# Hashed attention and expert layer: other layouts for turns and casts, moves and signs two pairs at a time, signs by bit operations, the uniform term by matmul

## The chip, the core and the metric

The kernel runs on one core of one Trainium2 chip. The metric is the device time of one execution in microseconds, the median of several runs. The core's engines are TensorE (PE, with PEld for its weight loads), VectorE (DVE), ScalarE (ACT), GpSimd (POOL) and SyncE (SP, which here only issues DMAs). They run side by side, each through its own list of instructions in a fixed order, and wait for one another by semaphores. An instruction that waits holds back everything behind it on its engine.

## What is computed

Attention over four batches, eight heads, 768 positions and 64 features, where a query sees only the keys with the same hash (the signs of six projections), and on its output a layer of eight low-rank experts, of which two are used per row.

```python
q_bits = (np.einsum('bhsd,dk->bhsk', q, proj) > 0)      # the same for k; 6 bits
mask = q_bucket[:, :, :, None] == k_bucket[:, :, None, :]
scores = np.where(mask, scale * np.matmul(q, k.transpose(0, 1, 3, 2)), -1e9)
attn = softmax(scores); attn_out = np.matmul(attn, v)   # exp, divided by sum + 1e-9
logits = x @ w_gate                                     # x: attn_out, 3072 x 512
# the two largest logits e, softmaxed to w:
out = x + sum_e w[e] * ((x @ A[e]) @ B[e])              # A[e]: 512x16, B[e]: 16x512
```

## The kernel before

The 32 (batch, head) problems are taken as 16 pairs `p` of heads, four pairs to a batch. The whole program is a hand-held list, `ORDER`: each word is a method and its numbers (`sc.9.2` is `sc(9, 2)`), and the list's order is the order of the instructions on every engine. No scheduler moves anything.

For each pair from 1 on, q and k come in by DMA (`l`, into `nat`, three buffers), 128 partitions of 768 floats per tensor. DVE turns them in blocks of 32x32 (`t`, L278, into `R`). POOL casts `R` to bf16 in the order in which the transposed operand needs it (`c`, L281, into `Rb`): it reads contiguously and writes every sixth bf16 element. Eight DMAs per pair (`mv`, L286) move blocks of `Rb` to their partitions in `aug`: rows 0 to 63 hold the features, one column per position. Pair 0 goes another way, without those DMAs: TensorE transposes (`ta`), copies (`tca`), casts into `aug` (`ca`, L250), hash matmuls (`ha`, L258) and signs (`sa`, L265).

The hash of a pair is eight f32 matmuls (`h`, L295, two instructions each), which read `R` with a step of 64 elements. DVE compares with zero (`sn`, L299) and scales by a per-partition number (`sm2`, L303); a DMA writes the signs to DRAM (`sdw`, L307), another reads them back as seven rows of `aug` (`sdr`, L310). The score matmul (`sc`, L339) then contracts 71 rows: 64 features, six signs of ±16 whose products add up to a large number only where all agree, and one constant row. For a mismatch the exponential of the score vanishes.

The scores are cut into 146 tiles, nine to a pair, of 1024 columns each, in three buffers of PSUM. ScalarE turns each into P (`ex`, L344, bf16, three buffers). Products with V (`pv`, L366) of a pair run among the scores of the next pair. For queries that see no key, each product starts from a tiny uniform term: POOL sums V (`vsum`, L319 to L323), TensorE spreads the sum over the rows (`uni`, L326), DVE copies it to SBUF (`ucopy`, L330) and, before each half pair, into the PSUM bank of the products (`seed`, L355). A half pair ends with `rec` and `norm` on DVE (L372, L382), which free the bank. POOL also casts V (`vcast`, L314) and the output (`xcast`, L401). The expert layer of a batch (`xturn`, `lzm`, `top`, `dif`, `sel`, `gexp`, `gate`, `zmul`, `delta`, `addx`, `store`) stands among the scores of later pairs, and for the last batch at the end. The last two pairs go in four groups of query blocks.

SP issues nearly all DMAs in list order: loads, the 120 moves, the sign transfers, the stores.

## Time and profile before

| | |
|---|---|
| time, median of 3 runs | 240.85 us (237.78 to 241.51) |
| the profiled execution | 237.42 us, span 235.6 us, mean granted clock of TensorE 0.878 |
| busy of the span | PE 184.8, DVE 159.1, ACT 147.6, POOL 162.4 us |
| the 146 exponentials (L344) | 142.9 us busy, 64.2 us idle before them |
| largest other groups | PE scores 101.5, POOL casts L281 88.5, PE products 58.4, PE hashes 33.1 us |
| DMAs issued by SP | 120 moves `aug<-Rb`, 15 `dr<-s`, 15 `aug<-dr`, 46 loads of q, k, v for pairs, stores, weights |

"Busy" is the time in which at least one instruction of the group ran. Idle time is put down to what ended it, by the semaphore that came last. The granted clock is a share of 2.4 GHz.

### The profile page before, as it was taken

How to read it: one execution, taken by the hardware profiler on the slowest of the kernel's cores; microseconds unless marked ns; L12 is line 12 of the kernel's file. 1: busy time of each engine (PE TensorE's matmuls, PEld its weight loads, DVE VectorE, ACT ScalarE, POOL GpSimd, SP SyncE). 2: the span in 40 equal slices, each digit the busy share in tenths (PEclk: the TensorE clock that was granted, in tenths of full speed). 3: DMA queues.
4: the chain of work that ended last, by engine and by line, in shares of the span. 5: the costliest groups of instructions: out<-in, count | busy, mean ns of one | idle time of the engine just before them, and what ended most of it. 6: DMA issues, size and time to landing. Idle time of an engine off the chain costs nothing.

```text
span 235.6 us, 5542 instructions
## 1 busy us (share of the span) xinstructions
PE 184.8 (78%) x2131; PEld 114.1 (48%) x2131; DVE 159.1 (68%) x364; ACT 147.6 (63%) x163; POOL 162.4 (69%) x168
## 2 busy tenths in 40 slices
...
GB/s 216 336 50 28 192 132 52 178 229 134 181 223 137 164 184 45 190 276 133 95 179 212 183 34 160 145 207 147 203 69 82 85 50 67 123 3 3 187 162 188
DMA packets 41495, 33.36 MB, mean 142 GB/s; under 512 B 25433, under 2 KB 38397, under 8 KB 41469
## 3 DMA queue, kind: packets, MB, share of 16 engines
...
HBM read 20.06 MB, written 7.03 MB: 115 GB/s over the span
## 4 chain that ended last, share of the span: by engine, by line
PE 25%; POOL 24%; DVE 18%; DMA 9%; SPq 9%; issue 9%; ACT 4%; ACTq 0%; DVEq 0%; POOLq 0%
POOL Rb L281 17%; PE s L339 10%; SPq L286 7%; PE v L366 6%; DVE aug L265 6%; ACT P L344 4%; DMA aug<-Rb 4%; PE n L295 3%; DVE acc L490 3%; POOL va L319 3%; DMA proj<-in_proj_dram 2%; DMA vn<-in_v_dram 2%; DVE R L278 2%; DMA aug<-dr 2%; POOL vs L323 1%
## 5 line engine op out<-in xcount | busy, mean ns | idle before, releaser
L344 ACT ACTIVATE P<-s 128x1024 bf16<-128x1024 f32 (+1 forms) x146 | 142.9, 1045 | 64.2 <-PE s L339 62.1
L339 PE MATMUL s<-aug 71*128 71x256 bf16 (+4 forms) x432 | 101.5, 337 | 16.3 <-DMA aug<-Rb 9.1
L281 POOL CAST Rb<-R 128x768 bf16<-128x768 f32 x30 | 88.5, 3032 | 11.5 <-DMA aug<-Rb 10.4
L339 PEld LDWEIGHTS <-aug 71*128 71x128 bf16 (+1 forms) x432 | 45.3, 130 | 59.1 <-issue 36.7
L366 PEld LDWEIGHTS <-P 128*128 128x128 bf16 x1152 | 53.7, 103 | 22.1 <-issue 13.5
L366 PE MATMUL v<-vb,P 128*128 128x65 bf16 x1152 | 58.4, 200 | 3.4 <-DVE v L355 2.0
L295 PE MATMUL n<-R,hst 128*32 128x192 f32 x240 | 33.1, 610 | 1.9 <-POOL Rb L281 1.3
L278 DVE STREAM_TRANSPOSE R<-nat 128x768 f32<-128x768 f32 x30 | 29.8, 997 | 4.1 <-POOL Rb L281 3.9
L401 POOL CAST xb<-x 128x768 bf16<-128x768 f32 (+1 forms) x18 | 13.6, 756 | 27.3 <-DVE x L382 20.3
L319 POOL TENSOR_TENSOR va<-vn 128x384 f32<-128x384 f32 x16 | 17.7, 1116 | 6.2 <-DMA vn<-in_v_dram 6.1
L490 DVE SCALAR_TENSOR_TENSOR acc<-n,rt,x 128x512 f32<-128x512 f32 x17 | 12.7, 749 | 12.6 <-PE n L486 12.1
L382 DVE TENSOR_TENSOR x<-v,ri 128x384 f32<-128x384 f32 x28 | 16.8, 600 | 0.7
L299 DVE TENSOR_SCALAR sg<-n 128x192 bf16<-128x192 f32 x15 | 5.2, 349 | 17.4 <-PE n L295 17.4
L355 DVE COPY v<-u 128x390 f32<-128x390 f32 x28 | 15.8, 564 | 0.6
L314 POOL CAST vb<-vn 128x768 bf16<-128x768 f32 x16 | 13.5, 850 | 0.7 <-PE v L366 0.7
L413 DVE COPY xT<-n 128x768 bf16<-128x768 bf16 (+1 forms) x18 | 8.7, 484 | 7.1 <-PE n L408 6.8
L250 POOL CAST aug<-R 64x128 bf16<-64x128 f32 (+2 forms) x14 | 12.3, 1010 | 0.7 <-ACT R L243 0.5
L295 PEld LDWEIGHTS n<-R,hst 128*32 128x32 f32 x240 | 7.0, 120 | 11.8 <-issue 3.5
L303 DVE TENSOR_SCALAR s<-sg,ssc 128x192 bf16<-128x192 bf16 x15 | 12.5, 833 | 0.2
L372 DVE RECIPROCAL ri<-v 128x6 f32<-128x6 f32 x28 | 6.3, 225 | 9.0 <-PE v L366 8.6
L408 PE MATMUL n<-ident_bf,xb 128*128 128x128 bf16 x92 | 8.4, 225 | 2.5 <-DVE rt L466 2.3
L326 PE MATMUL n<-vs,eps 128*128 128x130 bf16 x16 | 3.8, 238 | 7.6 <-POOL vs L323 7.0
...
## 6 DMA issues: line engine op xcount, KB each, us to landing
...
aug<-Rb SPq DMA_DIRECT2D x120, 48.0 KB
...
```

The costliest lines, as they stand in the source:

```text
L265: self.nc.vector.tensor_scalar(out=self.augt(slice(64, 82), h, i, e, u, n), in0=self.hb(h)[r, u * P:(u + n) * P].rearrange("d (u p) -> d u ...
L278: self.nc.vector.transpose(out=self.R[p % 2][:, i], in_=self.nat[p % 3][:, i])
L281: self.nc.gpsimd.tensor_copy(out=self.Rb[p % 2][:, :, i].rearrange("p h f (c t) -> p h t f c", t=T), in_=self.R[p % 2][:, i].rearrange("p ...
L286: (self.nc.sync, self.nc.gpsimd)[eng].dma_start(out=self.aug[p % 4][32 * f:32 * f + 32, :, 192 * a:192 * a + 192], in_=self.Rb[p % 2][32 * ...
L295: self.nc.tensor.matmul(out=hs[32 * j:32 * j + 32], lhsT=self.hst[:, f].rearrange("p b i -> p (b i)"), rhs=rhs, start=(f == 0), stop=(f == ...
L319: add(out=a, in0=vn[:, :, 0:3, :], in1=vn[:, :, 3:6, :])
L339: self.nc.tensor.matmul(out=self.Sb[n % 3][:, o:o + qw], lhsT=aug[rows, 2 * h + 1, kt::T], rhs=aug[rows, 2 * h, q0:q0 + qw], start=True, s ...
L344: self.nc.scalar.activation(out=self.Pt[p % 3][:, at:at + w], in_=self.Sb[n % 3][:, 0:w], func=ACT.Exp, scale=0.125)
L355: self.nc.vector.tensor_copy(out=self.pvv(p, g), in_=self.u[p % 2][:, g:g + 1, :].to_broadcast([P, T, D + 1]))
L366: self.nc.tensor.matmul(out=v[:, i, :], lhsT=self.Pt[p % 3][:, o:o + P], rhs=self.vb[p % 3][:, h, kt, :], start=False, stop=(kt == T - 1), ...
L382: self.nc.vector.tensor_tensor(out=x[:, :, c:c + D], in0=v[:, :, 0:D], in1=self.ri[g % 2].unsqueeze(2).to_broadcast([P, T, D]), op=ALU.mult)
L490: self.nc.vector.scalar_tensor_tensor(out=self.acc[(m // 2) % 3][:, m % 2, lo:hi], in0=self.bank(bank)[:, lo:hi], scalar=self.rt[g % 2][:, ...
```

## The change

- `c` walks `R` in the order of its output: it reads floats 64 elements apart and writes contiguous bf16. `h` reads runs of 32 contiguous floats and leaves its result in the order (t, c); the permutation is done by `sn`.
- `Rb` and `aug` hold two pairs per buffer (two buffers each, instead of two and four of one pair). A move and a sign transfer of an even pair carry that pair and the next; pair 1 goes alone. P has two buffers instead of three.
- Signs are made by one bit operation: the projections are negated, so a set bit is a negative number, and `bits` takes the upper half of the f32 in PSUM, keeps its sign bit and sets the other bits to 16.0. `sm2`, the constant row and the constants for them go; the scores contract 70 rows, and the exponential gets a bias of −192 (six products of 256, times 0.125).
- Pair 0 is laid out in the order in which its casts and signs come, so both write contiguously; its q is loaded in pieces of 256 bytes for that.
- The uniform term is written straight into the PSUM bank by a matmul (`uv`) before each half pair. `uni`, `ucopy` and `seed` go.
- `dif`, `sel` and `gate` are written as scalar_tensor_tensor.
- `ORDER` is another list.

```diff
-        self.Rb = r("Rb", 2, [2, 2, 2, 192], BF16)
+        self.Rb = r("Rb", 2, [2, 2, 2, 2, 192], BF16)
+        self.sg = r("sg", 2, [2, 192], U16)
+        self.aug = r("aug", 2, [8, S], BF16)
-        self.Pt = r("P", 3, [2 * T * S], BF16)
+        self.Pt = r("P", 2, [2 * T * S], BF16)
...
     def la(self, i, h, eng):
         (self.nc.sync, self.nc.scalar)[eng].dma_start(
-            out=self.natA[:, h, i], in_=self.qk[i][0, h].rearrange("(p t) d -> p (t d)", t=T))
+            out=self.natA[:, h, i].rearrange("p (t d) -> p t d", t=T),
+            in_=self.qk[i][0, h].rearrange(("(t p) d -> p t d", "(p t) d -> p t d")[i], t=T))
...
     def augt(self, rows, h, i, e, u, n):
-        return self.aug[0][rows, 2 * h + i].rearrange("d (p u e) -> d e u p", e=2, u=3)[:, e, u:u + n]
+        return self.aug[0][rows, 2 * h + i].rearrange("d (u e p) -> d e u p", e=2, u=3)[:, e, u:u + n]
...
+    def bits(self, out, in_):
+        self.nc.vector.tensor_scalar(out=out, in0=in_, scalar1=0x8000, scalar2=0x4180, op0=ALU.bitwise_and,
+                                     op1=ALU.bitwise_or)
+
     def sa(self, h, i, e, u, n):
         c = 2 * i + e
-        r = slice(32 * c, 32 * c + 18)
-        self.nc.vector.tensor_scalar(out=self.augt(slice(64, 82), h, i, e, u, n),
-                                     in0=self.hb(h)[r, u * P:(u + n) * P].rearrange("d (u p) -> d u p", u=n),
-                                     scalar1=self.thr[r], scalar2=self.mul[r], op0=ALU.is_gt, op1=ALU.mult)
+        hi = self.hb(h)[32 * c:32 * c + 6, u * P:(u + n) * P].bitcast(U16).rearrange("d (u p w) -> d u p w", u=n, w=2)
+        self.bits(self.augt(slice(64, 70), h, i, e, u, n).bitcast(U16), hi[:, :, :, 1])
...
     def c(self, p, i):
-        self.nc.gpsimd.tensor_copy(
-            out=self.Rb[p % 2][:, :, i].rearrange("p h f (c t) -> p h t f c", t=T),
-            in_=self.R[p % 2][:, i].rearrange("p h (t f c) -> p h t f c", f=2, c=32))
+        self.nc.gpsimd.tensor_copy(out=self.Rb[(p // 2) % 2][:, p % 2, :, i].rearrange("p h f (c t) -> p h f c t", t=T),
+                                   in_=self.R[p % 2][:, i].rearrange("p h (t f c) -> p h f c t", f=2, c=32))
 
     def mv(self, p, a, f, eng=0):
+        lo = 1 if p == 1 else 0
         (self.nc.sync, self.nc.gpsimd)[eng].dma_start(
-            out=self.aug[p % 4][32 * f:32 * f + 32, :, 192 * a:192 * a + 192],
-            in_=self.Rb[p % 2][32 * a:32 * a + 32].rearrange("d h i f x -> d (h i) f x")[:, :, f])
+            out=self.aug[(p // 2) % 2][32 * f:32 * f + 32, 4 * lo:8, 192 * a:192 * a + 192],
+            in_=self.Rb[(p // 2) % 2][32 * a:32 * a + 32, lo:2].rearrange("d j h i f x -> d (j h i) f x")[:, :, f])
 
     def h(self, p, f):
-        hs = self.Nb[:, 0:192].rearrange("m (c t) -> m c t", t=T)
         for j in range(4):
             h, i = divmod(j, 2)
-            rhs = self.R[p % 2][:, i, h, :].rearrange("p (t f c) -> p f c t", f=2, c=32)[:, f]
-            self.nc.tensor.matmul(out=hs[32 * j:32 * j + 32], lhsT=self.hst[:, f].rearrange("p b i -> p (b i)"),
-                                  rhs=rhs, start=(f == 0), stop=(f == 1), skip_group_check=True)
+            self.nc.tensor.matmul(out=self.Nb[32 * j:32 * j + 32, 0:192],
+                                  lhsT=self.hst[:, f].rearrange("p b i -> p (b i)"),
+                                  rhs=self.R[p % 2][:, i, h].rearrange("p (t f c) -> p f t c", f=2, c=32)[:, f],
+                                  start=(f == 0), stop=(f == 1), skip_group_check=True)
 
     def sn(self, p):
-        self.nc.vector.tensor_scalar(out=self.sg[p % 2], in0=self.Nb[:, 0:192], scalar1=0.0, scalar2=0.5,
-                                     op0=ALU.is_gt, op1=ALU.subtract)
+        hi = self.Nb[:, 0:192].bitcast(U16).rearrange("p (t c w) -> p c t w", t=T, w=2)[:, :, :, 1]
+        self.bits(self.sg[(p // 2) % 2][:, p % 2].rearrange("p (c t) -> p c t", t=T), hi)
...
+    def uv(self, p, g):
+        if p < N - 2:
+            v = self.vs[p % 2][:, g:g + 1, :].to_broadcast([P, T, D + 1])
+        else:
+            v = self.vs[p % 2].unsqueeze(2).to_broadcast([P, 2, len(GROUPS[g]), D + 1])
+        self.nc.tensor.matmul(out=self.pvv(p, g), lhsT=self.eps, rhs=v, start=True, stop=False, skip_group_check=True)
...
-        self.nc.vector.tensor_mul(out=self.sm["gw"][g % 2][:, 0:n], in0=self.sm["m"][g % 2][:, 0:n],
-                                  in1=self.sm["e"][g % 2][:, 0:n])
+        self.nc.vector.scalar_tensor_tensor(out=self.sm["gw"][g % 2][:, 0:n], in0=self.sm["m"][g % 2][:, 0:n], scalar=1.0,
+                                            in1=self.sm["e"][g % 2][:, 0:n], op0=ALU.mult, op1=ALU.mult)
...
+c.9.1 sc.50.0 rec.4.1 sc.50.1 top.0.0.0 mv.6.1.0 lzm.0.1.1.0.4.-1 norm.4.1 lzm.0.1.2.0.4.-1 c.9.0 ex.49 dif.0.0 lv.8
```

The last line is one of the new list: the last move of pairs 6 and 7 stands behind tile 49 or so; tile 54 is the first of pair 6.

Three places of the order, before and after. The first is DVE at the start, behind the copies of pair 0's transposes (`R_73`); `R_74` belongs to pair 1, `s_67` and `v` are hash results in PSUM. Before:

```order
L265 TENSOR_SCALAR aug_81<-s_67,thr,mul 18x128 x2
L278 STREAM_TRANSPOSE R_74<-nat_71 128x768
L265 TENSOR_SCALAR aug_81<-s_67,thr,mul 18x128 x4
L278 STREAM_TRANSPOSE R_74<-nat_71 128x768
L265 TENSOR_SCALAR aug_81<-s_67,thr,mul 18x128 x2
L265 TENSOR_SCALAR aug_81<-s_67,thr,mul 18x2x128 x2
L265 TENSOR_SCALAR aug_81<-v,thr,mul 18x3x128
L299 TENSOR_SCALAR sg_78<-n 128x192
L303 TENSOR_SCALAR s_80<-sg_78,ssc 128x192
L265 TENSOR_SCALAR aug_81<-v,thr,mul 18x3x128 x3
```

After:

```order
L259 STREAM_TRANSPOSE R_74<-nat_71 128x768
L242 TENSOR_SCALAR aug_79<-s_67 6x128
L259 STREAM_TRANSPOSE R_74<-nat_71 128x768
L242 TENSOR_SCALAR aug_79<-s_67 6x128 x2
L242 TENSOR_SCALAR aug_79<-s_67 6x2x128
L242 TENSOR_SCALAR aug_79<-s_67 6x128 x3
L242 TENSOR_SCALAR aug_79<-s_67 6x2x128
L242 TENSOR_SCALAR sg_77<-n 128x192
L242 TENSOR_SCALAR aug_79<-v 6x3x128 x4
```

The number of signs is the same; the second turn of pair 1 stands behind three single signs where it stood behind six, and the second operation on pair 1's signs (L303) is gone.

The second place is PE at the uniform term of pair 4 (`vs_90`, then `vs_86`). `s_65` to `s_67` are the three score buffers, `aug_84` and `aug_79` hold pair 4. Before:

```order
L339 MATMUL s_65<-aug_84 128x256
L326 LDWEIGHTS eps
L326 MATMUL n<-vs_90,eps 128x130
L339 LDWEIGHTS aug_84
L339 MATMUL s_67<-aug_84 128x256
```

After:

```order
L324 MATMUL s_67<-aug_79 128x256
L350 LDWEIGHTS eps
L350 MATMUL v<-vs_86,eps 128x390
L324 LDWEIGHTS aug_79
L324 MATMUL s_65<-aug_79 128x256
L324 LDWEIGHTS aug_79
L324 MATMUL s_67<-aug_79 128x256
L357 LDWEIGHTS P_94
L357 MATMUL v<-vb_84,P_94 128x65
```

The short matmul into the bank `n` became a wide one into the bank `v` of the products, directly ahead of the products (L357) and once for each half pair; two scores stand between.

The third place is SP, the transfers of pairs 6 and 7 (`Rb_75` into `aug_83` and `Rb_76` into `aug_84` before; `Rb_76` into `aug_80` after). Before:

```order
L286 DMA aug_83<-Rb_75 32x4x192
L286 DMA aug_84<-Rb_76 32x4x192 x2
L286 DMA aug_83<-Rb_75 32x4x192 x2
L286 DMA aug_84<-Rb_76 32x4x192
L272 DMA nat_72<-in_q_dram 128x2x384
L286 DMA aug_83<-Rb_75 32x4x192
L310 DMA aug_83<-dr_60 7x4x768
L286 DMA aug_83<-Rb_75 32x4x192
L286 DMA aug_84<-Rb_76 32x4x192 x2
```

After:

```order
L267 DMA aug_80<-Rb_76 32x8x192
L253 DMA nat_71<-in_q_dram 128x2x384
L267 DMA aug_80<-Rb_76 32x8x192 x4
L285 DMA dr_61<-sg_78 128x2x192
L267 DMA aug_80<-Rb_76 32x8x192 x2
L253 DMA nat_70<-in_q_dram 128x2x384
L290 DMA aug_80<-dr_61 6x8x768
L267 DMA aug_80<-Rb_76 32x8x192
```

Sixteen moves, two writes and two reads of signs became eight, one and one, each of twice the size.

## Rows read from the trace of the kernel before

**Rows 1.** The page, busy us (share of the span) and instructions of each engine.

```profile
PE 184.8 (78%) x2131; PEld 114.1 (48%) x2131; DVE 159.1 (68%) x364; ACT 147.6 (63%) x163; POOL 162.4 (69%) x168
```

**Rows 2.** Windows: stretch, length, busy PE PEld DVE ACT POOL, clock, DMA, GB/s.

```profile
0.00:18.00 18.00, 11.43 (x65) 4.01 (x69) 11.96 (x31) 3.21 (x8) 13.19 (x34) 0.71 0.59 197
18.00:28.80 10.80, 5.22 (x23) 2.13 (x24) 10.60 (x9) 3.98 (x4) 10.50 (x10) 0.66 0.45 119
28.80:224.00 195.20, 163.79 (x2017) 106.01 (x2015) 128.31 (x288) 139.75 (x149) 138.70 (x126) 0.91 0.48 136
224.00:235.60 11.60, 4.32 (x32) 1.96 (x32) 8.28 (x39) 0.68 (x4) 0.00 (x0) 0.73 0.47 173
```

**Rows 3.** Timeline of ACT: start us, length, instructions, [idle before <- releaser].

```profile
28.83 3.38 ACT L344 ACTIVATE P<-s 128x1024 bf16<-128x1024 f32 x3 [5.45 <-PE s L339]
...
142.29 10.32 ACT L344 ACTIVATE P<-s 128x1024 bf16<-128x1024 f32 x11 [0.67 <-PE s L339]
```

**Rows 4.** Waits within 28.8 to 224 us: total us, times, longest us.

```profile
ACT P L344 <- PE s L339: 55.0, 45, 5.4
...
PE s L339 <- DMA aug<-Rb: 9.1, 4, 3.3
...
PE n L326 <- POOL vs L323: 7.0, 4, 2.6
...
PE s L339 <- DMA aug<-dr: 4.2, 2, 3.0
...
PE v L366 <- DVE v L355: 2.0, 3, 1.1
```

**Rows 5.** Groups by line and shape: busy us, mean ns | idle before.

```profile
L281 POOL CAST Rb<-R 128x768 bf16<-128x768 f32 x30 | 88.5, 3032 | 11.5 <-DMA aug<-Rb 10.4 <-DVE gw L457 0.5 <-DVE s L303 0.3
L366 PE MATMUL v<-vb,P 128*128 128x65 bf16 x1152 | 58.4, 200 | 3.4 <-DVE v L355 2.0 <-DVE v L358 1.4
...
L355 DVE COPY v<-u 128x390 f32<-128x390 f32 x28 | 15.8, 564 | 0.6
...
L401 POOL CAST xb<-x 128x768 bf16<-128x768 f32 x14 | 12.0, 858 | 21.8 <-DVE x L382 20.3 <-PE s L339 1.6
...
L457 DVE TENSOR_TENSOR gw<-m,e 128x24 f32<-128x24 f32 x6 | 7.5, 1247 | 0.2 <-ACT e L453 0.2
...
L265 DVE TENSOR_SCALAR aug<-v,thr,mul 18x384 bf16<-18x384 f32 x4 | 6.2, 1558 | 0.1
L265 DVE TENSOR_SCALAR aug<-s,thr,mul 18x128 bf16<-18x128 f32 x8 | 6.0, 756 | 0.9 <-PE s L258 0.8
L250 POOL CAST aug<-R 64x384 bf16<-64x384 f32 x4 | 5.6, 1551 | 0.1
...
L299 DVE TENSOR_SCALAR sg<-n 128x192 bf16<-128x192 f32 x15 | 5.2, 349 | 17.4 <-PE n L295 17.4
...
L250 POOL CAST aug<-R 64x128 bf16<-64x128 f32 x8 | 4.9, 733 | 0.1
...
L326 PE MATMUL n<-vs,eps 128*128 128x130 bf16 x16 | 3.8, 238 | 7.6 <-POOL vs L323 7.0 <-DVE sg L299 0.7
...
L401 POOL CAST xb<-x 128x256 bf16<-128x256 f32 x4 | 1.6, 400 | 5.5 <-DVE x L391 2.2 <-PE n L408 1.9 <-DVE top L439 1.4
```

**Rows 6.** Timeline of PE: sets of eight f32 matmuls, columns as in rows 3.

```profile
7.01 0.42 PE L258 MATMUL s<-R,px 128*32 128x128 f32 x8 [1.14 <-DVE R L243]
...
15.12 1.17 PE L295 MATMUL n<-R,hst 128*32 128x192 f32 x8 [1.34 <-POOL Rb L281]
...
128.11 1.10 PE L295 MATMUL n<-R,hst 128*32 128x192 f32 x8
```

**Rows 7.** Windows over the three sets of rows 6, columns as in rows 2.

```profile
7.00:7.45 0.45, 0.44 (x9) 0.24 (x9) 0.16 (x1) 0.26 (x1) 0.06 (x1) 1.00 0.75 283
...
15.10:16.30 1.20, 1.17 (x8) 0.22 (x8) 1.18 (x2) 0.00 (x0) 1.14 (x2) 0.50 0.00 0
128.10:129.20 1.10, 1.10 (x10) 0.22 (x10) 1.04 (x2) 0.93 (x1) 0.56 (x1) 1.00 0.39 94
```

More of the change, by code (lines that the diff above doesn't have):

```diff
@@ L14 @@
 BF16 = mybir.dt.bfloat16
+U16 = mybir.dt.uint16
 AX = mybir.AxisListType
@@ L548 @@
-h.7.0 norm.4.1 ex.47 mv.6.2.0 sc.48.1 dif.0.0 h.7.1 sel.0.0 xcast.4.0 seed.5.0 sdr.6 sc.49.0 gexp.0.0 mv.6.2.1
-sc.50.2 ex.48 gate.0.0 sn.7 sc.50.0 zmul.0.0.0.0 sc.49.1 mv.7.3.0 gsum.0.0 t.8.1 pv.5.0.0.3 xturn.4.0.-1
-zmul.0.0.2.0 mv.7.3.1 ex.49 pv.5.0.0.4 zmul.0.0.1.0 sc.51.1 sc.50.1 xout.4.0.-1 sc.51.0 l.11.1 vcast.7 pv.5.0.0.0
-ex.50 sc.51.2 grec.0.0 mv.7.2.0 zturn.0.0.-1 pv.5.0.0.2 sc.52.0 wcast.1 zout.0.0.-1 lv.9 pv.5.0.0.1 t.9.0 ex.51
-sc.52.1 c.8.1 mv.7.1.0 pv.5.0.0.5 sc.53.2 uni.6 mv.7.0.1 rec.5.0 ex.52 ucopy.6 c.8.0 sc.54.1 norm.5.0 lv.8 sc.53.0
@@ L558 @@
-addx.0.0.2.-1 l.12.0 ex.59 sc.60.0 sc.60.2 pv.6.0.0.4 mv.8.1.1 pv.6.0.0.5 vsum.9.0 top.0.1.0 xturn.5.0.-1 sel.0.1
-dif.0.1 mv.8.2.1 ex.60 rec.6.0 sc.62.2 sc.62.0 xout.5.0.-1 mv.8.1.0 sc.62.1 sc.61.0 c.9.0 sc.61.1 norm.6.0 gexp.0.1
-h.8.0 ex.62 h.8.1 seed.6.1 mv.9.0.1 sc.63.2 gate.0.1 sc.63.1 ex.61 pv.6.1.1.1 mv.8.2.0 sn.8 zmul.0.1.2.0 sc.63.0
-pv.6.1.1.5 sm2.8 mv.8.3.0 zmul.0.1.0.0 uni.7 pv.6.1.1.2 sc.65.1 ex.63 ucopy.7 zmul.0.1.1.0 sdw.8 sc.64.0 t.10.1
-sc.64.1 l.10.0 pv.6.1.1.4 pv.6.1.1.3 ex.64 pv.6.1.1.0 mv.9.2.1 gsum.0.1 sc.65.2 sc.65.0 rec.6.1 mv.8.0.1
@@ L573 @@
-pv.8.0.0.0 ex.79 sc.78.0 t.12.0 pv.8.0.0.3 sc.78.1 vsum.11.1 sc.78.2 uni.9 sc.80.2 pv.8.0.0.2 ex.78 c.11.0
-pv.8.0.0.4 ucopy.9 sc.80.1 sc.80.0 lzm.1.0.0.0.4.-1 rec.8.0 norm.8.0 sc.82.0 vsum.10.1 ex.80 sc.82.1
-lzm.1.0.2.0.4.-1 vcast.10 seed.8.1 sc.81.2 lzm.1.0.1.0.4.-1 sc.81.0 ex.82 pv.8.1.1.3 lzo.1.0.-1 c.11.1 sc.81.1
-pv.8.1.1.2 pv.8.1.1.4 top.1.0.1 sm2.10 sc.83.1 ex.81 top.1.0.0 sc.83.0 top.1.0.2 sdw.10 sc.83.2 pv.8.1.1.0
-pv.8.1.1.1 mv.10.1.0 pv.8.1.1.5 h.11.0 ex.83 mv.10.3.1 rec.8.1 sel.1.0 dif.1.0 sc.84.0 norm.8.1 mv.10.0.0 sc.84.1
@@ L578 @@
-sc.84.2 h.11.1 gexp.1.0 seed.9.0 xcast.8.0 ex.84 sc.85.1 sdr.10 sc.86.1 gate.1.0 sn.11 sc.85.0 sc.86.2 mv.11.2.0
-zmul.1.0.0.0 sm2.11 pv.9.0.0.1 ex.85 t.12.1 sc.86.0 xturn.8.0.-1 vsum.10.2 mv.11.2.1 pv.9.0.0.4 zmul.1.0.2.0 lv.12
-pv.9.0.0.2 ex.86 xout.8.0.-1 pv.9.0.0.3 sc.87.2 zmul.1.0.1.0 l.14.0 sc.87.1 sc.87.0 c.12.0 pv.9.0.0.0 mv.11.1.0
-zturn.1.0.-1 ex.87 sc.88.0 mv.11.0.1 sc.89.0 zout.1.0.-1 sc.88.1 gsum.1.0 c.12.1 uni.10 pv.9.0.0.5 grec.1.0
-mv.11.3.0 sc.89.1 ex.88 ucopy.10 sc.89.2 rec.9.0 sdw.11 sc.90.0 norm.9.0 delta.1.0.0.-1 vsum.11.2 mv.11.3.1 sc.90.2
@@ L588 @@
-addx.1.0.2.-1 pv.10.0.0.3 ex.94 l.15.1 pv.10.0.0.4 sc.98.2 mv.12.2.0 c.13.1 sc.98.0 dif.1.1 sel.1.1 pv.10.0.0.2
-t.13.0 xturn.9.0.-1 gexp.1.1 ex.96 sc.98.1 pv.10.0.0.5 vsum.12.1 sc.97.0 gate.1.1 pv.10.0.0.1 c.13.0 gsum.1.1
-pv.10.0.0.0 xout.9.0.-1 ex.98 sc.97.1 sc.99.1 rec.10.0 sc.99.2 h.12.0 norm.10.0 zmul.1.1.2.0 mv.13.2.0 h.12.1 ex.97
-zmul.1.1.0.0 seed.10.1 mv.13.1.1 sc.99.0 sc.101.1 zmul.1.1.1.0 sn.12 sc.101.2 store.0.2.0 pv.10.1.1.1 ex.99 sm2.12
-uni.11 sc.100.1 mv.13.0.1 sc.100.0 ucopy.11 pv.10.1.1.5 mv.12.3.0 zturn.1.1.-1 ex.100 pv.10.1.1.2 sc.101.0 mv.12.0.1
```

341 lines of the change are left out of this document (169 added, 172 removed).

## The prediction

> **What bounds the kernel now.** I read the page's busy shares first, then the stages by windows, then ScalarE's timeline, the waits inside the long stage, and last the durations by shape. The shares name no single bound: PE 78%, POOL 69%, DVE 68%, ACT 63% [rows 1]. The stages do better [rows 2]. Up to 28.8 us only four of the 146 exponentials (L344) have run; DVE and POOL are busy 10.6 and 10.5 of the last 10.8 us there, and the granted clock is 0.66 of 2.4 GHz while PE is busy 5.2 us. From 28.8 to 224.0 us the other 142 run, PE busy 163.8 of 195.2 us at a mean granted clock of 0.91; the last 11.6 us are the end of the expert layer, mostly DVE. ScalarE is not the bound: once it ran eleven exponentials in 10.32 us, 0.94 each [rows 3], and 142 at that pace are 133 us of the 195. It waits 55.0 us in that stage for score matmuls [rows 4]. So PE and what feeds PE set the end: 163.8 us of PE work and 31.4 us of PE idle. Of that idle, PE's own rows name the moves of q and k into `aug` (9.1), the sign rows read back from DRAM (4.2), and the sum of V from POOL (7.0) [rows 4].
>
> The profiled execution took 237.4 us, 1.8 more than its span of 235.6. The sum is made against it; the median shown is 240.85, 1.4% above, so a median of the changed kernel may sit that much higher too.
>
> **The change, part by part.**
>
> *The start (28.8 us).* DVE's signs of pair 0 (`sa`, L265) write two-byte elements six columns apart: 756 ns for 128 columns, 1558 for 384. L299 writes 192 contiguous ones in 349, and the copy L355 writes 390 in 564 [rows 5]. The new `sa` writes contiguously, at most 0.35 and 0.56: eight and four of them fall from 12.2 us to 5.0. POOL's casts into `aug` (L250) make the same change of layout: 733 and 1551 ns, against 400 for 256 contiguous columns and 858 for 768 (L401), so 0.40 and about 0.52; 10.5 us become 5.3. The casts of pair 1 (L281) follow on POOL. Both chains shrink by 7 us or a little more, and either would end last, so I take 7.5 (4 if first loads, now in pieces of 256 bytes for q, come late; 11 if both chains and the two 256-wide forms fall together). The new order puts pair 1's turns ahead of some signs, as the old one does.
>
> *The cast `c` (L281).* 3032 ns for 768 elements, written two bytes wide and 12 bytes apart, 28 of its 30 behind 28.8 us. The new one reads four-byte elements 256 bytes apart and writes contiguously. No row of the trace has that. The bounds are 858 (L401, contiguous on both sides) and 3032 (as slow as now) [rows 5]; with one side mended I take the middle, 1.9. That frees 28 × 1.13 = 32 us of POOL's 138.7 in the stage; POOL is off PE's path except through the waits named above, so the gain is counted there. The Trainium skill (GPSIMD Engine Reference, Performance pitfalls for Q7 kernels) speaks against this edit: reads whose step is above 8 bytes cost about 2.9 cycles an element instead of 1.9. That half more, put on the 858 of the contiguous row, would give an estimate of 1.3 us and 48 us of POOL freed, and 1 us off the start; no row of this trace shows a strided read on POOL.
>
> *The hash (`h`, L295).* A set of eight takes 1.10 us at granted clock 1.00 (2.4 GHz) and 1.17 at 0.50 (1.2 GHz) [rows 6, 7]: its time does not follow the clock. The same kind of matmul on contiguous data (L258) took 0.42 for eight of 128 columns at clock 1.00 [rows 6, 7]; for 192 columns that is 0.63. The new `h` reads runs of 32 contiguous elements. 28 sets in the long stage × 0.47 = −13.2 us of PE (0 if runs of 32 do not help; −19 if 0.42 holds).
>
> *The uniform term.* `uni` (16 × 238 ns, 3.8 us [rows 5]), `ucopy` and 36 `seed` copies go; 36 `uv` matmuls come, 28 of 390 columns. Six L366 matmuls of 65 columns are as wide, at 58.4/1152 = 51 ns each [rows 5]: 0.30 us. 28 × 0.30 and eight narrower, 1.2, less 3.8, is +5.8 us of PE (0 to +8). DVE loses 15.8 us of seeds [rows 5], which nobody waited for but PE for 2.0 us [rows 4]; `uv` waits for `norm`, one step earlier, so −1.
>
> *Moves for two pairs.* 120 moves of 48 KB become 8 of 48 and 56 of 96, plus half the sign transfers. PE's waits for them are 13.3 us [rows 4]. Places where a pair can come late fall from 15 to 8, and the casts ahead of them shorten: 13.3 × 8/15 = 7.0, so −6.3 (0 to −13). The `uv` matmuls still need the sum of V; with 32 of 138.7 us taken out of POOL's queue ahead of it I take half of the 7.0, −3.5 (0 to −7).
>
> *The clock.* 0.91 leaves 9% of 163.8, 15 us, if PE's time followed it fully. Idle falls by 10.8 of 31.4, a third, so −5 (0 to −8).
>
> *The rest.* `sm2` goes, `sn` reads halves of words: DVE has 67 us idle in the stage, which hides either. The gating's new form (`dif`, `sel`, `gate`) may shorten six 1247 ns products (L457) [rows 5]; DVE's idle hides that too, and uncovered it is 7.5 us at most. Two buffers instead of three for P: V·P of a pair ends inside the next pair in the order, so nothing waits. The exponential's bias is a column read instead of a constant: nothing.
>
> Sum: 28.8 − 7.5 = 21.3; 195.2 − 13.2 + 5.8 − 1 − 6.3 − 3.5 − 5 = 172.0; 11.6 as before. That is 204.9, and with 1.8 outside the span 206.7: **207 us**.
>
> **The rivals.**
>
> *POOL gains nothing.* If reading apart is as slow as writing apart, `c` stays near 3.0. For it: the same access is only turned round. Against it: L299 on DVE reads PSUM and is quick where L265, with the same kind of source, is slow; what differs is the write. The start loses 2.3, the waits about half of their saving (5) and the clock half of its (2.5): 217 us.
>
> *Whole groups come late.* A move now waits for both casts of two pairs and carries twice the bytes; if each of the seven later groups stops PE for the longest wait of today, 3.3 us [rows 4], that is 23 us where I put 7.0, and the clock gives nothing: 207 + 16 + 5 = 228. For it: the new order leaves two to four exponentials between the last transfer of a group and its first score, the old one mostly three to five. Against it: today's moves are late because they stand behind casts, which shorten.
>
> *Everything is covered.* No wait for moves (−7), contiguous sets at 0.42 (−6): 194 us. For it: ScalarE's eleven in a row show that PE can feed it at 0.94 when nothing is late.
>
> *Slower.* `uv` stands in PE's own queue behind DVE's `norm`; scores behind it cannot pass. Before, PE waited 2.0 us in all for 28 seeds, under 0.1 each. The change would have to cost 1.0 us at each of 36 `uv`s to take back the gain and pass 242 us (237.4 + 2%). The order puts four or more score matmuls between the last product and `uv` at 31 of the 36 and none at one, so I give it little.
>
> **How the numbers follow.** Forecast 0.52 (its own range 199 to 214), POOL gains nothing 0.13, groups late 0.16, all covered 0.15, slower 0.04. Two in ten outside gives 193 to 225. A measurement of this kernel tells about 2% from no change. Faster by over 2% means under 232.7: the forecast, the covered case, the slow cast and two thirds of the late groups, 0.90; within 2% 0.06; slower 0.04.
>
> **What would show it.** The fifth exponential near 21 us; L281's successor between 1.3 and 2.5 us; a set of eight hash matmuls near 0.6 at clock 1.00; `uv` near 0.3 with no wait on DVE above a few us in all; PE's waits for `aug` near 7 us, at even pairs only; a mean clock above 0.93 in the long stage. If PE's idle stays at 31 us while POOL and DVE idle more, the reading that they feed PE's waits is wrong. If PE's busy time stays at 164 us, the hash term is.

## The result and the profile after

The changed kernel took 190.99 us, the median of three runs (190.85 to 196.34), against 240.85: a ratio of 0.798 (0.776 to 0.820). In two later sets of rounds, each beside the kernel before, the ratio was 0.794 (0.789 to 0.800) and 0.820 (0.813 to 0.827). The forecast was 207 us, and the result lies 2 us under the range's lower end of 193.

Executions of one kernel here differ by some 5% with the clock that TensorE is granted, so quick executions are compared with quick ones where there are any, and the 0.820, from rounds in which only one of six executions of the changed kernel was quick (189.7 us), is no level to compare with below. Differences in us below are taken from ratios to the kernel before where there are two. The rows of after are those of a profile with span 187.9 us (189.7 us in all).

First the page's busy shares, for [rows 1].

```profile
PE 164.0 (87%) x2150; PEld 112.8 (60%) x2150; DVE 107.2 (57%) x286; ACT 151.3 (81%) x163; POOL 114.7 (61%) x168
```

Then windows, columns as in [rows 2]: the start, the stretch from the fifth exponential to the end of the last (the long stage; before it began at 28.8 us and was 195.2 us long), and the part of it in which ScalarE runs nearly without a gap.

```profile
0.00:18.00 18.00, 11.81 (x70) 5.68 (x71) 7.56 (x22) 3.19 (x8) 9.59 (x36) 1.00 0.68 219
...
22.05:176.64 154.59, 145.36 (x2041) 104.36 (x2034) 87.70 (x223) 143.43 (x150) 101.32 (x127) 0.97 0.63 176
...
50.00:180.00 130.00, 120.27 (x1737) 88.78 (x1735) 78.93 (x220) 120.05 (x128) 78.41 (x103) 1.00 0.57 159
```

TensorE's busy time in the long stage fell from 163.8 to 145.4 us and its idle time from 31.4 to 9.2; DVE has 41 us less work there and POOL 37 us less. From 50 to 180 us TensorE and ScalarE are busy equally long, 120 of 130 us.

ScalarE's timeline, as in [rows 3] (line 328 is the exponential now):

```profile
17.95 5.13 ACT L328 ACTIVATE P<-s,bias 128x1024 bf16<-128x1024 f32 x5 [3.47 <-PE s L324]
23.39 1.11 ACT L328 ACTIVATE P<-s,bias 128x1024 bf16<-128x1024 f32 x1 [0.32 <-PE s L324]
...
31.52 27.43 ACT L328 ACTIVATE P<-s,bias 128x1024 bf16<-128x1024 f32 x27 [1.18 <-PE s L324]
60.32 14.17 ACT L328 ACTIVATE P<-s,bias 128x1024 bf16<-128x1024 f32 x14 [1.38 <-PE s L324]
...
81.51 26.36 ACT L328 ACTIVATE P<-s,bias 128x1024 bf16<-128x1024 f32 x26
...
175.53 1.11 ACT L328 ACTIVATE P<-s,bias 128x1024 bf16<-128x1024 f32 x1 [1.89 <-PE s L324]
```

The fifth exponential starts at 17.95 + 4 x 1.03 = 22.05 us, where it started at 28.83. Then 27 and 26 follow each other without a gap; before, the longest such row was 11. One alone takes 1.11 us now, in a row 1.016; before it was 0.94 in a row.

The waits of the long stage, for [rows 4]: nearly all are gone. ScalarE waits 8.1 us for scores instead of 55.0, and no wait of TensorE's matmuls names the moved pairs or the sum of V (its weight loads wait 0.6 us for moved pairs).

```profile
ACT P L328 <- PE s L324: 8.1, 7, 2.3
PE s L324 <- ACT P L328: 2.5, 6, 0.8
...
PE s L324 <- DMA wst<-in_moe_w_gate_dram: 1.2, 1, 1.2
PE s L324 <- DMA vn<-in_v_dram: 1.0, 1, 1.0
```

The changed operations by shape, for [rows 5] (line 262 is the cast, 392 a cast that reads and writes contiguously, 350 the uniform term, 242 signs, 229 the first casts):

```profile
L262 POOL CAST Rb<-R 128x768 bf16<-128x768 f32 x30 | 45.7, 1540 | 5.2 <-DMA aug<-Rb 3.4 <-DVE top L430 0.8 <-DVE R L259 0.8
...
L392 POOL CAST xb<-x 128x768 bf16<-128x768 f32 x14 | 11.6, 827 | 21.0 <-DVE x L373 13.4 <-DMA aug<-Rb 5.9 <-PE n L274 1.5
...
L350 PE MATMUL v<-vs,eps 128*128 128x390 bf16 x28 | 9.7, 348 | 0.1
...
L242 DVE TENSOR_SCALAR aug<-s 6x128 uint16<-6x128 uint16 x8 | 2.3, 286 | 1.8 <-PE s L237 1.6
L229 POOL CAST aug<-R 64x128 bf16<-64x128 f32 x8 | 2.3, 290 | 3.6 <-DVE R L222 3.5
L242 DVE TENSOR_SCALAR aug<-v 6x384 uint16<-6x384 uint16 x4 | 2.2, 555 | 0.1
L229 POOL CAST aug<-R 64x384 bf16<-64x384 f32 x4 | 2.0, 503 | 0.1
```

And sets of eight hash matmuls (line 274) on TensorE's timeline, for [rows 6]: 0.43 us each at 36.38 (16 in 0.86) and 0.53 at 47.62, where the clock is 2.4 GHz, and 0.87 at 24.68, where it is 1.2. Before, a set took 1.10 and 1.17 at the two levels [rows 6, 7].

```profile
24.68 0.87 PE L274 MATMUL n<-R,hst 128*32 128x192 f32 x8
...
36.38 0.86 PE L274 MATMUL n<-R,hst 128*32 128x192 f32 x16
47.62 0.53 PE L274 MATMUL n<-R,hst 128*32 128x192 f32 x8
```

### The profile page after: what moved, and what is told of

Read it like the earlier page. It is cut to its first block, busy times and chain, and to the rows that moved or that the text cites. A ratio compares the mean times of both kernels' runs of the same rounds, so it can differ in the third digit from the quotient of the medians.

```text
span 194.5 us, 5393 instructions
## 1 busy us (share of the span) xinstructions
PE 170.3 (88%) x2143; PEld 115.9 (60%) x2150; DVE 106.8 (55%) x286; ACT 152.1 (78%) x163; POOL 114.5 (59%) x168
## 4 chain that ended last, share of the span: by engine, by line
PE 41%; ACT 17%; DVE 12%; DMA 12%; issue 9%; SPq 4%; POOL 3%; ACTq 1%; DVEq 0%; POOLq 0%
PE s L324 19%; ACT P L328 17%; PE v L357 10%; DMA vn<-in_v_dram 4%; DMA aug<-Rb 4%; DVE acc L483 3%; PE n L274 3%; DMA nat<-in_k_dram 3%; SPq L267 2%; POOL Rb L262 2%; PE v L350 2%; DVE R L259 2%; DMA dr<-sg 1%; DVE aug L242 1%; PE n L418 1%
## 5 line engine op out<-in xcount | busy, mean ns | idle before, releaser
L328 ACT ACTIVATE P<-s,bias 128x1024 bf16<-128x1024 f32 (+1 forms) x146 | 148.0, 1144 | 18.9 <-PE s L324 17.9
L324 PE MATMUL s<-aug 70*128 70x256 bf16 (+2 forms) x432 | 106.1, 334 | 7.7 <-ACT P L328 2.8
L357 PEld LDWEIGHTS <-P 128*128 128x128 bf16 x1152 | 55.7, 103 | 15.9 <-issue 5.3
L357 PE MATMUL v<-vb,P 128*128 128x65 bf16 x1152 | 61.3, 200 | 0.4
L324 PEld LDWEIGHTS <-aug 70*128 70x128 bf16 x432 | 45.6, 128 | 26.1 <-issue 18.4
L262 POOL CAST Rb<-R 128x768 bf16<-128x768 f32 x30 | 45.5, 1534 | 10.7 <-DVE R L259 6.5
L274 PE MATMUL n<-R,hst 128*32 128x192 f32 x240 | 17.2, 374 | 0.6 <-DVE xT L404 0.4
L294 POOL CAST vb<-vn 128x768 bf16<-128x768 f32 x16 | 13.2, 826 | 3.2 <-PE s L324 3.2
L350 PE MATMUL v<-vs,eps 128*128 128x390 bf16 (+2 forms) x36 | 12.1, 336 | 0.8 <-DVE x L382 0.7
L462 POOL TENSOR_TENSOR zm<-lz,gw 128x128 bf16<-128x128 f32 x18 | 7.0, 401 | 9.0 <-DVE gw L450 8.8
L242 DVE TENSOR_SCALAR sg<-n 128x192 uint16<-128x192 uint16 x15 | 5.2, 348 | 11.4 <-PE n L274 11.4
L418 PEld LDWEIGHTS <-xT 128*128 128x128 bf16 x96 | 7.1, 98 | 2.5 <-issue 0.7
L229 POOL CAST aug<-R 64x128 bf16<-64x128 f32 (+2 forms) x14 | 5.0, 366 | 5.9 <-DVE R L222 4.2
```

Source lines behind the costliest of these rows:

```text
L262: self.nc.gpsimd.tensor_copy(out=self.Rb[(p // 2) % 2][:, p % 2, :, i].rearrange("p h f (c t) -> p h f c t", t=T), in_=self.R[p % 2][:, i] ...
L274: self.nc.tensor.matmul(out=self.Nb[32 * j:32 * j + 32, 0:192], lhsT=self.hst[:, f].rearrange("p b i -> p (b i)"), rhs=self.R[p % 2][:, i, ...
L294: self.nc.gpsimd.tensor_copy(out=self.vb[p % 3][:, :, :, 0:D], in_=self.vn[p % 2])
L324: self.nc.tensor.matmul(out=self.Sb[n % 3][:, o:o + qw], lhsT=lhsT, rhs=rhs, start=True, stop=True)
L328: self.nc.scalar.activation(out=self.Pt[p % 2][:, at:at + w], in_=self.Sb[n % 3][:, 0:w], func=ACT.Exp, scale=0.125, bias=self.bias)
L350: self.nc.tensor.matmul(out=self.pvv(p, g), lhsT=self.eps, rhs=v, start=True, stop=False, skip_group_check=True)
```

## The experiments

**Three pieces, each undone in the changed kernel.** The changed kernel ran beside them.

> The changed kernel as it is, as the level to which the other three runs of this chip are compared. 191 us, and a profile in which the granted clock of the long stage is nearer to 1 than the 0.93 of the profile at hand: then the stretch from 15 to 50 us, in which that profile had the clock at 0.5 to 0.6, is shorter, and the stretch behind it goes at 1.01 us for one exponential, as there.

191.62 us, ratio 0.794. The low stretch of the clock was expected to be shorter in its profile; but the granted clock is 0.50 from 20 to about 51 us, where in the profile above that lasts from about 22 to 32. The pace behind it is the same.

The old cast:

```diff
-    out=self.Rb[...].rearrange("p h f (c t) -> p h f c t", t=T),
-    in_=self.R[...].rearrange("p h (t f c) -> p h f c t", f=2, c=32)
+    out=self.Rb[...].rearrange("p h f (c t) -> p h t f c", t=T),
+    in_=self.R[...].rearrange("p h (t f c) -> p h t f c", f=2, c=32)
```

> The changed kernel with the cast's old access: read contiguous, written with strides; nothing else differs, the order neither. The 30 casts go from 1.53 to 3.03 us, 45 us more for GpSimd, which then has 140 of 156 us in the long stage. Theory one, GpSimd's relief is what took away TensorE's idle time: the waits for moved pairs come back and the time goes up by 12 us or more, to over 203 us. Theory two, the idle time went because the moves are half as many and the order is another: GpSimd has room enough for the old cast, and the time stays under 196 us.

215.09 us, ratio 0.904 (0.898 to 0.910): 0.110 x 237.6 = 26 us more. GpSimd is busy 147 of 214 us. The waits for moved pairs, which the first answer expected, don't come back by name: the largest of TensorE's waits is for other work of GpSimd's queue. The cast in the page's groups, that wait, and the window of the long stage:

```profile
L262 POOL CAST Rb<-R 128x768 bf16<-128x768 f32 x30 | 81.5, 2821 | 2.5 <-DVE R L259 2.1
```

```profile
PE n L399 <- POOL xb L392: 6.0, 4, 2.7
```

```profile
26.14:203.01 176.87, 158.70 (x2041) 110.87 (x2042) 91.41 (x221) 145.70 (x149) 129.92 (x125) 0.88 0.53 152
```

The fifth exponential starts 4.1 us later, at 26.14. In the long stage TensorE is idle 18.2 us where it was 9.2, and for the same matmuls busy 158.7 where it was 145.4, at a mean clock of 0.88 instead of 0.97. So half of the price is not idle time but slower work.

The old hash access:

```diff
-    matmul(out=self.Nb[32 * j:32 * j + 32, 0:192],
-           rhs=self.R[...].rearrange("p (t f c) -> p f t c", f=2, c=32)[:, f])
+           rhs=self.R[...].rearrange("p (t f c) -> p f c t", f=2, c=32)[:, f])
     # and the signs read and written as they lie
```

> The changed kernel with the hash matmuls' old access: moving operand read from every sixth group with a stride, hash bits read and written contiguous. A set of eight goes from 0.46 to 1.10 us, 0.64 x 30 = 19 us more for TensorE. If TensorE's time is what the long stage is made of, as the prediction took it, the time goes up by nearly all of it, to 207 to 210 us; if ScalarE is the bound of the middle, TensorE has 8 us free in the long stage and the time goes up by 8 to 13 us only, to 199 to 204 us.

200.7 us, ratio 0.841 (0.835 to 0.848): 11 us more. The hash has 32.3 us again instead of the 17.2 in the profile of after_again, so 15 were added and 11 reached the end. It is the second answer of the two.

```profile
L274 PE MATMUL n<-R,hst 128*32 128x192 f32 x240 | 32.3, 596 | 0.0
```

The moves of one pair:

```diff
+    # mv, sdw and sdr: one transfer for each pair of the two, both on sync
-    self.nc.sync.dma_start(out=self.aug[...][32*f:32*f+32, 4*lo:8, ...], ...)
+    self.nc.sync.dma_start(out=self.aug[...][32*f:32*f+32, 4*lo:4*lo+4, ...], ...)
+    if not lo:
+        self.nc.sync.dma_start(out=self.aug[...][32*f:32*f+32, 4:8, ...], ...)
```

> The changed kernel with each transfer for two pairs split in two of one pair, behind each other on the same queue; the order is the same. The prediction took 6.3 us as the gain from half as many moves. If that holds: 195 to 199 us, with waits of the scores for moved pairs in the list of waits. If moves are hidden now by the work of two pairs: within 2 us of the changed kernel.

218.19 us, ratio 0.906 (0.897 to 0.915): against the changed kernel's 0.794 and 0.798 that is 26 to 27 us, four times the 6.3 predicted. TensorE's waits name the moved pairs and signs again; the window of the long stage stands behind them:

```profile
PE s L329 <- DMA aug<-Rb: 11.5, 3, 5.7
PE s L329 <- DMA aug<-dr: 5.5, 2, 2.9
```

```profile
22.30:202.93 180.63, 158.69 (x2035) 111.38 (x2034) 87.27 (x223) 145.59 (x150) 101.18 (x127) 0.86 0.54 151
```

The long stage is 26.0 us longer than in the changed kernel: 12.7 us of it are idle time of TensorE (21.9 us), and 13.3 are its busy time, at a mean clock of 0.86 instead of 0.97. Again half of the price is slower work; how much of that is the clock and how much that matmuls overlap less behind gaps is not separated here.

SyncE's timeline ahead of one such place (start, length; SPq is its queue of issues):

```profile
77.23 0.59 SPq L271 DMA_DIRECT2D aug<-Rb  x1
77.91 0.54 SPq L253 DMA_DIRECT2D nat<-in_q_dram  x1
78.51 0.58 SPq L267 DMA_DIRECT2D aug<-Rb  x1
79.14 0.59 SPq L271 DMA_DIRECT2D aug<-Rb  x1
...
90.04 0.60 SPq L271 DMA_DIRECT2D aug<-Rb  x1
90.73 0.55 SPq L256 DMA_DIRECT2D vn<-in_v_dram  x1
```

What TensorE's timeline has at its end, and the windows around it:

```profile
93.46 1.03 PE L329 MATMUL s<-aug 70*128 70x512 bf16 x2 [5.70 <-DMA aug<-Rb]
```

```profile
77.00:88.00 11.00, 10.61 (x163) 8.40 (x160) 9.20 (x23) 11.00 (x13) 10.08 (x14) 1.00 0.36 96
88.00:94.00 6.00, 0.54 (x2) 0.32 (x3) 1.30 (x5) 0.69 (x1) 1.10 (x3) 0.72 0.74 209
```

SyncE issues from 77.23 to 91 us without a gap, 0.64 us from one move to the next, moves, signs and loads in the order of the list; TensorE runs out of scores and stands for 5.7 us. The DMA engines themselves are busy 0.36 until 88 us, while the queue is worked off, and 0.74 from 88 to 94, when the last moves land among loads: for the most part it is the issuing, not the moving, and the runs on SyncE's queue below tell the two apart.

**The pieces together.** Old cast and single moves; all three; and the other way round, in the kernel before, the new cast alone and with the new hash.

> The changed kernel with the old cast and the single-pair moves together. Alone the old cast cost 24 us and the single moves 26 us. If they are two separate charges on the end: 238 to 243 us. If both make the same thing late, the moved pair for the next scores, and each alone is long enough to show: 216 to 228 us.

> The changed kernel with the old cast, the old hash matmuls and the single-pair moves: what is left of the change is the order, the signs made with bit operations, the uniform term on TensorE, contraction of 70 rows and the bias. The three undone singly cost 24, 10 and 26 us. If they add up: 245 to 252 us, slower than the kernel before. If they hide each other: 222 to 236 us. How far the time lies below the kernel before, in the same rounds, is what the rest of the change is worth without them.

> The kernel before with the new cast alone. With the new hash matmuls beside it the gain was 23 us (215 us). If the hash matmuls count for their own 19 us of TensorE's time there, as the prediction took it: 230 to 236 us. If the cast makes most of it, since GpSimd was what made the moves late: 216 to 224 us.

> The kernel before, with two things of the change alone: the cast reads float32 with strides and writes contiguously, and the hash matmuls read and write contiguous runs (the strided read of their result is then done where the sign is taken). The order, the moves of one pair and all the rest are those of before. Undone singly in the changed kernel they gave back 24 and 10 us of 47. Theory one, these two accesses are most of the change whatever the order: 203 to 210 us. Theory two, the gain needs the order that was made for them, because in the old order the moves are issued late and one by one: over 218 us.

The first took 236.38 us (232.03 to 237.57; the kernel before 238.36 in the same rounds), between the two answers: the two charges of about 26 us add up for the most part. The second took 236.75, ratio 0.996 (0.989 to 1.003): the old hash added nothing clear to that, and all the rest of the change, the order among it, is worth nothing measurable without the three pieces. Undone singly the three cost 26, 26 and 11 us, more than the whole gain, so no piece has a share of its own. In the kernel before, the new cast alone gave 221.31 us, 17 us less, as the second answer had it, and with the new hash 215.28, ratio 0.894 (0.886 to 0.903), 25 us less. Expected was over 218 or under 210; it lies between. In b_casthash TensorE still waits 14.8 us for moves, against 9.1 before, and 14% of the chain that ended last is SyncE issuing, against 9%. I read that as SyncE making them late once GpSimd is quicker; no run changes it alone in the old order.

**What SyncE's queue costs.** Two runs tell the issuing from the landing in two transfers: one adds small transfers behind the moves, one issues the second transfer from GpSimd.

```diff
+    if not lo:   # x_spq, behind each move of two pairs
+        self.nc.sync.dma_start(out=self.scr[self.k:self.k + 1], in_=self.ident[0:1, 0:64])
-        self.nc.sync.dma_start(out=self.aug[...][..., 4:8, ...], ...)     # u_movesq, second pair
+        self.nc.gpsimd.dma_start(out=self.aug[...][..., 4:8, ...], ...)
```

> The changed kernel with one more transfer of 256 bytes on SyncE's queue behind each of the 56 two-pair moves, from a constant to a row of its own in DRAM that nobody reads. The moves themselves stay as they are. Theory one, what the single-pair moves cost is SyncE's time for the issues, 0.6 us each, in front of the loads and moves behind them: 56 x 0.6 = 34 us more on that queue, and the time goes up by 12 us or more, over 203 us. Theory two, it is the landing of a pair in two transfers: the small ones pass unseen, 190 to 195 us.

> The changed kernel with each two-pair move split in two as in the run with single moves, but the second of them issued by GpSimd instead of SyncE (the signs' transfers split and on SyncE as there). Theory one, SyncE's queue was the cause of the 26 us: with 56 issues less on it most of this is gone unless GpSimd, with 115 of 194 us busy, becomes late in its place: 195 to 208 us. Theory two, the landing in two transfers is the cause: 214 to 220 us as before.

x_spq took 206.99 us, ratio 0.871 (0.858 to 0.883): 56 transfers of 256 bytes, which nothing reads, cost 17 to 18 us against 0.798 and 0.794. Each holds SyncE for some 0.45 us, 25 us in all, as two neighbours on its timeline show:

```profile
70.94 0.59 SPq L268 DMA_DIRECT2D aug<-Rb  x1
71.58 0.45 SPq L272 DMA_DIRECT2D scr<-ident  x1
```

The profile of that run puts 8.5 us of TensorE's waits down to these small transfers themselves, so a part of the price may be their landing and not their issue; this run doesn't tell.

From GpSimd's queue the second transfers (u_movesq) gave 204.41 us, ratio 0.859 (0.843 to 0.876): the wait for moved pairs fell from 11.5 to 0.9, though each pair still lands in two transfers, and some 11 of the 26 to 27 us came back. GpSimd, which each issue keeps busy, is what TensorE waits for now; the page's group first, then TensorE's waits:

```profile
L271 POOL DMA_DIRECT2D aug<-Rb x56 | 31.1, 559 | 0.3 <-POOL Rb L262 0.3
```

```profile
PE n L404 <- POOL xb L397: 7.3, 4, 2.8
PE s L329 <- DMA aug<-Rb: 0.9, 1, 0.9
```

Together the two speak for the queue.

**What bounds the kernel now.** The bias as a number; the uniform term left out, so that the first product opens the sum; both.

```diff
-    scale=0.125, bias=self.bias)          # x_imm, x_immnouv
+    scale=0.125, bias=-192.0)
-    matmul(out=self.pvv(p, g), lhsT=self.eps, rhs=v, start=True, stop=False)   # x_nouv, x_immnouv
```

> The changed kernel with the exponential's bias as an immediate number instead of a column of SBUF; the output stays the same. Theory one, ScalarE is the bound of the middle of the changed kernel, and the column is what made its exponentials slower: one alone takes 1.02 us again instead of 1.11, the pace in a row goes from 1.01 us to 0.94, and about 0.07 x 120 = 8 us are gained, 183 us. Theory two, the column costs nothing on the path, because the scores would be late next: the pace is as of TensorE, over 1.0 us, and the time stays at 190 to 191 us.

> The changed kernel without its uniform term: the matmuls of eps and vs that open each accumulation are left out, and the first product of probabilities with v opens it. 36 matmuls of 0.34 us, 12.1 us in all, go from TensorE. If TensorE's time is what bounds the changed kernel, as the prediction's 0.30 us net for each of them has it, about 9 us are gained, 182 us; if ScalarE bounds the stretch from 50 to 180 us, only the ones outside of it count: 187 to 190 us.

> The changed kernel with the bias as an immediate number and without the uniform term: what took 10 us from ScalarE and what took 12 us from TensorE, together; each alone moved the end by nothing. Theory one, the two engines hold each other, both being 93 to 96% busy from 50 to 180 us: together 8 to 10 us are gained, 180 to 184 us. Theory two, a third thing (moves, loads, GpSimd, or the clock) is as late as they are: 187 to 192 us, with the waits of the scores on that thing in the list.

x_imm took 195.72 us (192.33 to 197.02), no better than the 191.62 (188.74 to 198.78) beside it. ScalarE was faster, 1.02 us for one and 17.90/19 = 0.942 in a row, 142.3 us busy instead of 152.5; it then waited for scores, and TensorE's mean clock from 50 to 110 us was 0.91 instead of 0.97. Its timeline, and its wait within 50 to 180 us, which in after_again, of the same rounds, is 5.8:

```profile
97.08 17.90 ACT L328 ACTIVATE P<-s 128x1024 bf16<-128x1024 f32 x19 [0.18 <-PE s L324]
```

```profile
ACT P L328 <- PE s L324: 13.4, 16, 2.2
```

x_nouv took 192.6 us, ratio 0.810 (0.782 to 0.839): TensorE without 12 us of its work, and no gain. Both together (x_immnouv) took 192.21, so it isn't that the two engines alone hold each other. At one place of that run, TensorE's timeline and windows:

```profile
60.21 0.28 PE L324 MATMUL s<-aug 70*128 70x256 bf16 x1 [3.50 <-DMA wst<-in_moe_w_gate_dram]
```

```profile
58.00:62.40 4.40, 2.19 (x20) 0.89 (x21) 1.08 (x2) 0.00 (x0) 3.50 (x3) 0.89 1.00 240
62.40:66.00 3.60, 3.60 (x39) 2.63 (x38) 0.14 (x1) 3.07 (x3) 0.70 (x2) 0.50 0.86 244
66.00:70.00 4.00, 4.00 (x46) 2.15 (x44) 1.44 (x4) 2.38 (x3) 2.66 (x3) 0.72 0.02 4
```

TensorE, now ahead, waits for a transfer, and behind the wait the clock is at 1.2 GHz for nearly 7 us in which it has no gap at all: what was gained is given back twice. In the whole run the clock was 0.94 and 0.95 from 50 to 110 and 110 to 180 us; in the profile of the result it is 1.00 and 0.99.

**The clock at the start, and loads on another queue.** Idle matmuls into unused columns (x_fill, which also has eleven warm-up matmuls instead of six); the same with the bias as a number and an earlier load of k (x_best); then 22 loads issued by GpSimd (x_loads); then everything together (x_all).

```diff
+    def fill(self, n):    # x_fill, x_best, x_all: in the order ahead of sc.1.0, sc.4.0 and sc.3.1
+        matmul(out=self.Nb[:, 256:512], lhsT=self.wz[:, 0:P], rhs=self.wz[:, 0:256])
-    la.0.0.0 lproj la.1.0.1    # x_best, x_all
+    la.0.0.0 la.1.0.1 lproj
-    self.nc.sync.dma_start(out=self.vn[...])   # and wst, bst: x_loads, x_all
+    self.nc.gpsimd.dma_start(out=self.vn[...])
```

> The changed kernel with idle matmuls added on TensorE, into columns of the bank n that nothing else uses: five more of 512 columns at the start, and 10, 3 and 9 of 256 columns ahead of the scores at 16 to 22 us, where TensorE waits for the first pair and for the first exponentials. They compute nothing that is used. Theory one, the granted clock falls to 0.5 at 20 us because TensorE has been idle in half of the 6 us before: with the gaps filled it stays at 1.0, and the 22 to 30 us at half clock, in which TensorE has no idle time at all, shrink by up to a third: 182 to 187 us. Theory two, the fall has another cause: the clock shows 0.5 from about 20 us as before, and the time is 191 us or more.

> The changed kernel with three edits together: the bias as an immediate number, the idle matmuls of the other run at 16 to 22 us, and the load of k ahead of those of proj on ScalarE's queue as in the kernel before. The immediate alone took 10 us off ScalarE's time and nothing off the end, with the clock at 0.89 to 0.91 in all its runs. If the clock is what took its gain: with the clock kept up, 178 to 183 us. If TensorE's own work bounds the middle as soon as ScalarE is faster: 186 to 190 us.

The windows of x_fill, and of the changed kernel in the profile of the result:

```profile
18.00:50.00 32.00, 28.39 (x336) 18.76 (x333) 14.37 (x25) 26.26 (x26) 24.40 (x28) 0.89 0.80 223
```

```profile
18.00:50.00 32.00, 29.68 (x343) 17.97 (x342) 16.09 (x29) 27.85 (x28) 26.69 (x30) 0.84 0.79 220
```

With the gaps filled the clock stayed at 2.4 GHz from 16 to 38 us, and in x_best too it didn't fall at 20 to 22 us, as it did in all three profiles of the changed kernel. So it was the gaps that let the clock fall there. In both runs it fell at 39 us instead, in x_fill at a wait of 2.4 us for moved pairs. The time gained nothing by it, 192.04 us, ratio 0.803 (0.795 to 0.810): the changed kernel is as fast where its clock comes back by 32 us, as in the profile of the result, and behind 50 us the pace is ScalarE's. x_best took 190.62, ratio 0.799 (0.791 to 0.807), not to be told from the changed kernel.

> The changed kernel with the 16 loads of v and the 6 of the adapter weights issued by GpSimd instead of SyncE, at the same places of the order. SyncE has 22 issues of some 0.5 us less; GpSimd, at 115 of 190 us, has them more. If SyncE's queue holds the changed kernel even as it is: 182 to 187 us. If it holds it only where ScalarE and TensorE have been made faster: within 2 us of the changed kernel in the same rounds, a little worse if GpSimd becomes late.

> The same loads on GpSimd's queue, with the immediate bias, the idle matmuls at 16 to 22 us, and the load of k ahead of those of proj. If SyncE's queue is what took the gain of the faster exponential: 178 to 184 us, with no wait of the scores for a transfer over 1 us. If not: 187 to 191 us, as these three edits gave with all loads on SyncE.

203.09 us (199.85 to 207.04) and 198.26 (193.85 to 201.98), where the changed kernel in the same rounds had 194.93 (189.70 to 198.97; 189 to 192 was expected of it). Both are slower than either answer had it. A load of V issued by GpSimd keeps it busy for 0.74 us, so what SyncE is spared GpSimd pays for; which wait took the time isn't shown. No version beat the changed kernel.

## Why the prediction was wrong, and where it was right

Span against span, 187.9 us were measured and 204.9 predicted. Of the 17.0 us between them, 11.4 are idle time of TensorE in the long stage (9.2 us, predicted 31.4 - 10.8 = 20.6), 6.0 are its busy time (145.4, predicted 151.4), and the start and the end cancel to 0.4.

**The step that failed is the one on the moves.** It took TensorE's rows of waits, 13.3 us, and scaled them by the places where a pair can come late, 15 to 8: -6.3. In the same way it took half of the wait for V's sum, -3.5, and -1 of the seeds' 2.0. By these two profiles the rows were right and the scaling was wrong. The waits for moves, signs, V's sum and seeds (9.1, 4.2, 7.0 and 2.0) are 22.3 us; none of them is left among the waits of TensorE's matmuls, and the idle time fell by 22.2 us where 10.8 were taken. The 9.2 us that are left are as much as all other idle time was before.

Counting places takes every place that is left to be as late as before; the shorter casts, which the step names, have no number in it. A wait in TensorE's rows is only where the lateness ends. It is made on two queues that run in order: SyncE, which needs some 0.6 us for the issue of a move, 120 of them before and 64 now, and GpSimd with 88.5 us of casts [rows 5]. Both were busy well under the whole span (SyncE's 218 issues make some 122 of 235.6 us before, its 148 now some 78 of 187.9), and on average had time; but a move that stands behind a cast, and a load that stands behind eight moves, is late all the same. With either queue as long as before, 26 to 27 us (moves) or 26 us (cast) come back. I counted places and should have counted the queue. That GpSimd is "off PE's path except through the waits named above" was wrong too: the old cast costs its 26 us without a single wait of TensorE's for moves or V's sum.

**The clock** was taken as -5. Of the 18.4 us by which TensorE's busy time fell, the hash makes 30.8 - 14.9 = 15.9 and the uniform term takes back 11.5 - 3.8 = 7.7, by the sums of their groups. Some 10 are left, while the clock went from 0.91 to 0.97. They aren't separated from the overlap of matmuls; most of the 6.0 us error in busy time lies here. It hangs on the step above: the -5 is 15 us times the third of the idle time that was to go, and with the 22.2 of 31.4 us that went the same rule gives 10.6. The moves and the cast, undone, show the same from the other side: half of the price of each is slower work.

**"ScalarE is not the bound"** held for the kernel before and fails for the new one: from 31 to 172 us it runs in rows of up to 27. The claim was no term of the sum. **"The exponential's bias: nothing"** was wrong as to the instruction, 0.09 us alone and 0.07 in a row, 10 us of ScalarE's time, and x_imm shows no gain in time when that is taken away. The Trainium skill (ScalarE: Activation LUTs, What ACT_TABLE_LOAD costs) puts a pointer operand at some 93 ns. The 1.11 against 1.02 us here agree.

**The start**: 22.05 us for the fifth exponential where 21.3 was taken. The signs at 286 and 555 ns and the casts at 290 and 503 came out as estimated or faster. The first exponential didn't move (17.95 after 17.98), since the load of k now stands behind those of proj and TensorE first waits for it until 6.9 us (in x_best, with that load ahead again, until 4.2, and the first exponential starts at 17.00); the four behind it followed at once.

**The cast** came to 1.54 us, 1.9 taken. The Trainium skill's rule (GPSIMD Engine Reference, Performance pitfalls for Q7 kernels), half more for a read with a wide step, gave an estimate of 1.3; beside 0.83 for contiguous data (line 392) the trace has 0.71 more, so the rule's direction holds and its size is too small. **The hash** came to 0.43 to 0.53 for a set at full clock, 0.63 taken, and -15.9 us of TensorE against -13.2; 11 of it show at the end. **The uniform term** took 0.348 us and +7.7, where 0.30 and +5.8 were taken, with a single wait on DVE, 0.7 us at a narrow one; at the end it costs nothing that x_nouv shows. **The gating's new form** isn't what shortened the products of 1247 ns to 241: in b_casthash the old form takes 289, and in u_cast one product of the new form takes 2.85 us again.

The rival that came true was "everything is covered", at 194 us. Its argument, that eleven exponentials in a row show what TensorE can do when nothing is late, was the best evidence in the profile; 0.15 was too little for it. Its -7 for the moves came true; with the other halves for V's sum and the seeds, 3.5 and 1.0, which it left in place, it makes the 11.4 us of idle time. Its -6 for the hash is luck: the sets gave only 2.7 more than the forecast had, the uniform term took 1.9 more, and the clock, with what isn't separated from it, gave 5.2 more. The other rivals are refuted: the cast gained, no group came late, and the time fell.
